# The attention's 1 / rms on GpSimd: one power operation in place of eleven Newton-step operations

## Chip, core and metric

The kernel runs on one core of a Trainium2 chip. The metric is the device time of the whole program in microseconds. A core has five engines with queues of their own: TensorE (PE in the profile, its weight loads PEld), VectorE (DVE), ScalarE (ACT), GpSimd (POOL) and SyncE (SP, which here issues every DMA). Each engine works through its queue in order and waits on semaphores where it needs another's result.

## What is computed

A linear attention, whose normalised output goes through a gated MLP that mixes tokens. Eight batches of 576 tokens; 8 heads of 64 channels, so 512 channels; the MLP is 512 to 1024 to 512.

```
kv   = einsum('bhsd,bhse->bhde', k, v)
out  = einsum('bhsd,bhde->bhse', q, kv)
rms  = sqrt(mean(out * out, axis=-1) + 1e-06)
x    = out / rms * g_norm                     # heads joined to 512 channels
h    = gelu(x @ w_in);  u, v = halves of h
v_n  = layer_norm(v) * g_ln
v_s  = einsum('ts,bsd->btd', w_sg, v_n) + b_sg[None, :, None]
y    = x + (u * v_s) @ w_out
```

## The kernel before

Matrices are multiplied in float32 quality from two parts: a rounded high part (names ending in h) and a rest (ending in o). `split` makes them: ScalarE casts the high part, VectorE or GpSimd subtracts to get the rest. A product is then three matmuls, high by high, high by rest and rest by high.

Each batch b has an attention object `Att` and an MLP object `Moe`. Attention: `kv` sums key by value over five chunks of tokens in the PSUM tile pkv; `o` makes po for each pair of heads, squares it (sq, ScalarE) and scales it by g into x; `sums` adds the squares per head with a matmul by a matrix of ones into pss; `rstd` turns pss into ry, the 1 / rms, 128 partitions by 144. Batch 0 spreads ry over the channels on TensorE: `scale_pe` makes yh and y_parts and then eight matmuls pb, whose results multiply x. The other batches write ry to DRAM (rd) and read it back broadcast (bc for 512 tokens, bl for the last 64), and `scale` and `xleft` multiply x with them. `xsplit` makes xh and xo.

MLP: `v` makes pv, gelu (hv), layer norm and its parts vh and vo; its 1 / sigma, rs, is an addition and a power on GpSimd, on 128x1, with the exponent tile mhalf (-0.5). `uu` makes pu and u. `s_main` and `s_left` make pg, the token mix; VectorE scales it into gt, GpSimd multiplies it with u, and it is split into gh and go. `out` makes py and adds it to x. Weights w_in and w_out are 64-bit words that are converted on chip (`w64`, tiles "words" and w64: ScalarE L164, VectorE L166 to L168, GpSimd's addition L169, and a split); w_u, w_v, w_out give wuh/wuo, wvh/wvo, woh/woo, and ws the token-mixing weights wsh/wso.

The work is written down step by step in the lists FIRST (batch 0 with all weight work and batch 1's attention), ODD, EVEN, LAST_EVEN and LAST; in each, step r (or F, or T for later batches) is `rstd` of this or the next batch. The list is not the queues' order: the framework's scheduler lays the instructions of all engines out by its own simulated clock, and the queues follow that. The tiles rm, ry and ra have one buffer each, shared by all batches.

Of the kernel before, what the change touches and what calls it, by code (L numbers as in the profile page):

```python
# [9 lines left out]
I32 = mybir.dt.int32  # L10
U32 = mybir.dt.uint32
AF = mybir.ActivationFunctionType
ALU = mybir.AluOpType

P = 128
B, H, S, D = 8, 8, 576, 64
# [7 lines left out]
QS = S // NQ  # L24
ZO = H - 2
RMS_EPS = 1e-6
LN_EPS = 1e-6
MAGIC = 0x5F3759DF
# [43 lines left out]
def tile_linear_attn_gmlp(  # L72
# [18 lines left out]
    nc = tc.nc  # L91
# [4 lines left out]
    def T(shape, dtype, tag, bufs=1, nm=None):  # L96
        return sb.tile(shape, dtype, tag=tag, bufs=bufs, name=nm or tag)
# [21 lines left out]
    mhalf = T([P, 1], F32, "mhalf")  # L119
# [65 lines left out]
    class Att:  # L185
# [106 lines left out]
        def rstd(self):  # L292
            m = T([P, QS], F32, "rm")
            y = T([P, QS], F32, "ry")
            a = T([P, QS], F32, "ra")
            v = nc.vector
            v.tensor_scalar(m, self.pss[:, :QS], D * RMS_EPS, None, op0=ALU.add)
            v.tensor_scalar(a.bitcast(I32), m.bitcast(I32), 1, None, op0=ALU.logical_shift_right)
            v.tensor_scalar(y.bitcast(I32), a.bitcast(I32), -1.0, float(MAGIC), op0=ALU.mult, op1=ALU.add)
            for _ in range(3):  # L300
                v.tensor_tensor(a, y, y, op=ALU.mult)
                v.scalar_tensor_tensor(a, a, -0.5, m, op0=ALU.mult, op1=ALU.mult)
                v.scalar_tensor_tensor(y, a, 1.5, y, op0=ALU.add, op1=ALU.mult)
            if self.b == 0:
                self.y = y
            else:
                self.rd = dr.tile([32, S], F32, tag="rd", name="rd")
                nc.sync.dma_start(self.rd.rearrange("h (j t) -> j h t", j=NQ), y)
# [342 lines left out]
```

## Time and profile before

| | |
|---|---|
| median of 2 runs | 562.2 us (561.58 to 562.82) |
| profiled execution | 561.72 us |
| its span | 559.9 us, 9943 instructions |
| mean granted TensorE clock | 0.982 |
| DMA traffic | 55.50 MB |

Engine rows of the profile give busy us, share of the span and instructions. Group rows give line, engine, operation, tiles out<-in with shapes and count, then busy us and mean ns of one, then the engine's idle time before them. Timeline rows give start us, duration us, engine, line, operation. Rows of a line or tile give least/median/greatest ns of one operation. Rows of a stretch give from:to, its length, the busy us (and count) of PE, PEld, DVE, ACT and POOL, the granted clock, the DMA engines' share and GB/s. Rows of the chain that ended last give start us, duration us, engine, tile, line and count.

### The profile page before, as it was taken

The page shows a single profiled execution, that of the slowest core. Times are in us where ns is not written, and L with a number is a line of the kernel's source. Part 1 is how long each engine was busy: PE and PEld are TensorE (multiplying, and loading weights), DVE is VectorE, ACT ScalarE, POOL GpSimd, SP SyncE. Part 2 cuts the span into 40 slices and gives each one's busy share as a digit, 9 for nine tenths or more (in the row PEclk, how much of TensorE's full clock was granted, in tenths as well). Part 3 has the DMA queues.
Part 4 walks back from the last instruction along what each step waited for, and adds up shares of the span by engine and source line. Part 5 has one row for each costly group of instructions (what it writes and reads, how often), then busy time and mean ns, then how long its engine had stood idle before and what let it go on. Part 6 is the DMA issues. An engine that isn't in the chain of part 4 may idle for free.

```text
span 559.9 us, 9943 instructions
## 1 busy us (share of the span) xinstructions
PE 523.3 (93%) x3944; PEld 469.3 (84%) x3944; DVE 305.6 (55%) x644; ACT 200.5 (36%) x457; POOL 196.3 (35%) x221
## 2 busy tenths in 40 slices
PE   2878957999999999899999999999999999999997
PEld 2556756888998988898998989988898979989997
DVE  0689989834645263844634353663652444762443
ACT  1446636432434332342414352332513342421210
POOL 1217667341249022422248131331328312430221
PEclk9979979999999999999999999989999999999999
DMA  8996556332023302513044312613242202102002
GB/s 221 293 332 189 164 160 165 116 100 86 22 70 85 123 28 64 162 32 128 22 134 110 127 43 53 188 39 108 60 115 73 85 1 53 37 2 85 1 1 86
DMA packets 33723, 55.50 MB, mean 99 GB/s; under 512 B 7308, under 2 KB 9228, under 8 KB 33676
## 3 DMA queue, kind: packets, MB, share of 16 engines
q1 hardware_dynamic: 33676, 54.86, 32.6%
q8 instruction: 31, 0.51, 0.4%
q14 instruction: 16, 0.13, 0.1%
HBM read 44.90 MB, written 9.95 MB: 98 GB/s over the span
## 4 chain that ended last, share of the span: by engine, by line
PE 61%; DVE 15%; DMA 13%; POOL 4%; ACT 2%; issue 2%; SPq 2%; POOLq 0%; DVEq 0%
PE py L454 18%; PE pv L386 13%; PE pu L413 12%; PE pg L427 10%; DMA bc<-rd 5%; PE po L266 4%; DMA kv_first<-in_kx 3%; PE pss L281 2%; DVE xo L111 2%; DVE go L111 2%; SPq L314 2%; DMA rd<-ry 1%; POOL x L321 1%; PE pkv L220 1%; DVE words L166 1%
## 5 line engine op out<-in xcount | busy, mean ns | idle before, releaser
L440 POOL TENSOR_TENSOR gt<-gt,u 128x288 f32<-128x288 f32 x64 | 55.6, 884 | 93.8 <-DVE gt L439 85.3
L427 PE MATMUL pg<-wsh,vh 128*128 128x288 f32 x256 | 77.5, 305 | 1.8 <-ACT vh L110 1.8
L454 PE MATMUL py<-go,woh 128*128 128x288 f32 x256 | 75.5, 299 | 2.2 <-DVE go L111 2.1
L454 PE MATMUL py<-gh,woh 128*128 128x288 f32 x256 | 73.0, 304 | 4.1 <-ACT gh L110 3.8
L427 PE MATMUL pg<-wso,vh 128*128 128x288 f32 x256 | 75.9, 299 | 0.0
L427 PE MATMUL pg<-wsh,vo 128*128 128x288 f32 x256 | 74.0, 299 | 1.6 <-DVE vo L111 1.6
L454 PE MATMUL py<-gh,woo 128*128 128x288 f32 x256 | 74.8, 296 | 0.0
L376 POOL TENSOR_SCALAR rs<-mv 128x1 f32<-128x1 f32 x32 | 9.8, 307 | 144.3 <-DVE mv L375 144.1
L111 DVE TENSOR_TENSOR go<-gt,gh 128x288 fp32r<-128x288 f32 x64 | 40.0, 638 | 28.2 <-ACT gh L110 28.2
L457 DVE SCALAR_TENSOR_TENSOR x<-py,x 128x288 f32<-128x288 f32 x64 | 28.2, 454 | 45.2 <-PE py L454 45.0
L427 PEld LDWEIGHTS pg<-wsh,vh 128*128 128x128 f32 x256 | 49.0, 192 | 4.3 <-ACT vh L110 2.4
L454 PEld LDWEIGHTS py<-gh,woh 128*128 128x128 f32 x256 | 46.6, 189 | 7.2 <-ACT gh L110 5.0
L413 PE MATMUL pu<-xh,wuh 128*128 128x288 f32 x256 | 48.0, 305 | 4.2 <-ACT hv L370 3.7
L454 PEld LDWEIGHTS py<-go,woh 128*128 128x128 f32 x256 | 48.5, 189 | 3.4 <-DVE go L111 3.3
L427 PEld LDWEIGHTS pg<-wsh,vo 128*128 128x128 f32 x256 | 48.1, 192 | 2.7 <-DVE vo L111 2.3
L439 DVE SCALAR_TENSOR_TENSOR gt<-pg,glt,b_bc 128x288 f32<-128x288 f32 x64 | 30.8, 511 | 34.6 <-PE pg L437 34.1
L427 PEld LDWEIGHTS pg<-wso,vh 128*128 128x128 f32 x256 | 49.3, 193 | 0.3
L454 PEld LDWEIGHTS py<-gh,woo 128*128 128x128 f32 x256 | 48.6, 190 | 0.0
L413 PE MATMUL pu<-xh,wuo 128*128 128x288 f32 x256 | 46.1, 298 | 2.3 <-POOL wuo L111 2.3
L413 PE MATMUL pu<-xo,wuh 128*128 128x288 f32 x256 | 46.3, 299 | 1.6 <-DVE xo L111 1.6
L416 ACT ACTIVATE u<-pu 128x288 f32<-128x288 f32 x64 | 26.2, 411 | 60.0 <-PE pu L413 59.9
L110 ACT CAST gh<-gt 128x288 fp32r<-128x288 f32 x64 | 26.9, 434 | 57.1 <-POOL gt L440 42.6
(117 smaller groups left out, 1076.8 us busy)
## 6 DMA issues: line engine op xcount, KB each, us to landing
q<-in_qT SPq DMA_DIRECT2D x32, 288.0 KB, 3.5
out_y<-x SPq DMA_DIRECT2D x28, 288.0 KB, 2.1
bc<-rd SPq DMA_DIRECT2D x28, 256.0 KB, 4.3
k<-in_kx SPq DMA_DIRECT2D x24, 256.0 KB, 4.1
v<-in_vx SPq DMA_DIRECT2D x24, 256.0 KB, 4.3
kv_first<-in_kx SPq DMA_DIRECT2D x8, 256.0 KB, 7.2
kv_first<-in_vx SPq DMA_DIRECT2D x8, 256.0 KB, 8.4
words<-in_wu SPq DMA_DIRECT2D x4, 512.0 KB
```

What stands on the lines that cost most here:

```text
L110: nc.scalar.copy(hi, src)
L111: return (lo_engine or nc.vector).tensor_tensor(lo, src, f32(hi), op=ALU.subtract)
L266: nc.tensor.matmul(po[:, :HS], a, m[:, t], start=(i == 0), stop=(i == len(terms) - 1))
L281: nc.tensor.matmul(self.pss[32 * j : 32 * j + m, :QS], ones[:, ZO - 2 * p : ZO - 2 * p + m], self.sq[p, j // 2][:, j % 2 * QS : (j % 2 + 1 ...
L386: nc.tensor.matmul(pv, a(cc), w[:, cc, :], start=(n == 0), stop=(n == 11))
L413: nc.tensor.matmul(pu[:, :HS], w[:, cc, f], a[cc][:, t], start=(n == 0), stop=(n == 11))
L416: nc.scalar.activation(u, pu[:, :HS], AF.Gelu_apprx_tanh, scale=W_UP)
L427: nc.tensor.matmul(ps[:, :HS], a[:, d], w[:, c, t], start=(n == 0), stop=False)
L439: nc.vector.scalar_tensor_tensor(gt, ps[:, :HS], glt[:, dc : dc + 1], b_bc[:, t], op0=ALU.mult, op1=ALU.add)
L440: nc.gpsimd.tensor_tensor(gt, gt, self.u.pop((j, dc)), op=ALU.mult)
L454: nc.tensor.matmul(po[:, :HS], w[:, dc, f], a, start=(i == 0), stop=(i == 11))
L457: nc.vector.scalar_tensor_tensor(x[:, t], po[:, :HS], W_UP, x[:, t], op0=ALU.mult, op1=ALU.add)
```

## The change

`rstd` keeps its first operation (VectorE adds the epsilon to pss, giving rm). The other eleven go: two that make a first guess from the bits, and three Newton steps of three operations each. One GpSimd operation raises rm to the power -0.5, with the one-column tile mhalf broadcast along 144.

```
             v = nc.vector
-            v.tensor_scalar(m, self.pss[:, :QS], D * RMS_EPS, None, op0=ALU.add)
-            v.tensor_scalar(a.bitcast(I32), m.bitcast(I32), 1, None, op0=ALU.logical_shift_right)
-            v.tensor_scalar(y.bitcast(I32), a.bitcast(I32), -1.0, float(MAGIC), op0=ALU.mult, op1=ALU.add)
-            for _ in range(3):
-                v.tensor_tensor(a, y, y, op=ALU.mult)
-                v.scalar_tensor_tensor(a, a, -0.5, m, op0=ALU.mult, op1=ALU.mult)
-                v.scalar_tensor_tensor(y, a, 1.5, y, op0=ALU.add, op1=ALU.mult)
+            nc.vector.tensor_scalar(m, self.pss[:, :QS], D * RMS_EPS, None, op0=ALU.add)
+            nc.gpsimd.tensor_tensor(y, m, mhalf.to_broadcast([P, QS]), op=ALU.pow)
             if self.b == 0:
                 self.y = y
```

The scheduler lays out the whole program anew with this. Lines behind the edit have numbers lower by five. On VectorE, at the start of the program, behind batch 0's rm there stood the Newton steps, then yh and y_parts:

```order
L302 SCALAR_TENSOR_TENSOR ra<-ra,rm 128x144
L237 COPY kvf<-pkv 64x4x64
L303 SCALAR_TENSOR_TENSOR ry<-ra,ry 128x144
L328 CAST yh<-ry 128x144
L331 SCALAR_TENSOR_TENSOR y_parts<-yh,ext,ry 32x144 x4
```

Now, from batch 1's kvf on:

```order
L166 TENSOR_SCALAR words<-words 128x256
L168 SCALAR_TENSOR_TENSOR w_522<-words,w_522 128x256
L167 TENSOR_SCALAR w_542<-w_542 128x256
L168 SCALAR_TENSOR_TENSOR w_542<-words,w_542 128x256
L242 TENSOR_TENSOR kvo<-pkv,kvh 64x4x64
L323 CAST yh<-ry 128x144
L297 TENSOR_SCALAR rm<-pss 128x144
L242 TENSOR_TENSOR kvo<-pkv,kvh 64x4x64
L326 SCALAR_TENSOR_TENSOR y_parts<-yh,ext,ry 32x144 x4
L167 TENSOR_SCALAR w_460<-w_460 128x512
L335 TENSOR_TENSOR x<-x,pb 128x288
```

Twelve weight conversions (the last four of them shown; w_522 and w_542 are of w_out, w_460 of w_v) and the first half of batch 2's kvo now stand ahead of yh, and batch 1's rm right behind it.

On GpSimd, at the start, the weight additions and x splits were:

```order
L111 TENSOR_TENSOR wuo<-w_382,wuh 128x2x256
L169 TENSOR_TENSOR w_428<-w_428,words 128x512
L169 TENSOR_TENSOR w_470<-w_470,words 128x512
L111 TENSOR_TENSOR xo<-x,xh 128x576 x2
L169 TENSOR_TENSOR w_495<-w_495,words 128x512
```

and are now (ry is the power, of batch 0 and of batch 1):

```order
L298 TENSOR_TENSOR ry<-rm,mhalf 128x144
L111 TENSOR_TENSOR wuo<-w_372,wuh 128x2x256
L169 TENSOR_TENSOR w_418<-w_418,words 128x512
L169 TENSOR_TENSOR w_522<-w_522,words 128x256
L169 TENSOR_TENSOR w_542<-w_542,words 128x256
L298 TENSOR_TENSOR ry<-rm,mhalf 128x144
L169 TENSOR_TENSOR w_460<-w_460,words 128x512
L111 TENSOR_TENSOR xo<-x,xh 128x576
L111 TENSOR_TENSOR wso<-stage,wsh 128x576 x2
L111 TENSOR_TENSOR xo<-x,xh 128x576
```

Both powers stand ahead of the second w_v addition and of batch 0's x splits. In a later odd batch (3) VectorE's order around rm is, with buffer numbers, now:

```order
L373 TENSOR_SCALAR hv_2135<-hv_2135,mv_2138,rs_2139 128x512
L297 TENSOR_SCALAR rm_2186<-pss_2117 128x144
L369 BN_STATS st_2162<-hv_2160 128x6
L111 TENSOR_TENSOR vo_2051<-hv_2135,vh_2050 128x512
L370 BN_AGGR mv_2163<-st_2162 128x2
L369 BN_STATS st_2337<-hv_2335 128x6
L370 BN_AGGR mv_2338<-st_2337 128x2
L373 TENSOR_SCALAR hv_2160<-hv_2160,mv_2163,rs_2164 128x512
```

and on GpSimd rs_2164, for which the last row waits, stands behind the power (before, no GpSimd operation belonged to `rstd`, and the Newton steps stood between these rows on VectorE).

## Prediction

> **What bounds the kernel now.** I read the page's busy shares first, then the slices, then a table of stretches.
>
> ```profile
> PE 523.3 (93%) x3944; PEld 469.3 (84%) x3944; DVE 305.6 (55%) x644; ACT 200.5 (36%) x457; POOL 196.3 (35%) x221
> PE   2878957999999999899999999999999999999997
> 25.00:57.00 32.00, 26.83 (x248) 18.68 (x249) 29.93 (x56) 18.40 (x45) 15.46 (x11) 0.89 0.81 258
> 57.00:105.00 48.00, 38.35 (x249) 31.78 (x249) 44.02 (x85) 25.42 (x55) 29.36 (x29) 0.93 0.53 150
> 130.00:560.00 430.00, 419.78 (x3122) 387.38 (x3120) 212.21 (x459) 142.08 (x328) 137.96 (x163) 0.99 0.24 71
> ```
>
> There are two regimes. From 130 us on TensorE (PE) is busy 419.78 of 430 us: it sets the time, and VectorE (DVE, the third pair) is half idle. From 25 to 105 us DVE is the full engine (29.93 of 32, 44.02 of 48 us) and PE idles 5.2 + 9.7 us. So a relief of DVE is worth something before 105 us only; after that the change matters by whether it makes PE wait.
>
> **What goes.** Of twelve DVE operations per batch on 128x144 one stays.
>
> ```profile
> L302 DVE SCALAR_TENSOR_TENSOR ra<-ra,rm 128x144 f32<-128x144 f32 x24 | 9.5, 398 | 0.7
> L301 DVE TENSOR_TENSOR ra<-ry 128x144 f32<-128x144 f32 x24 | 7.8, 324 | 0.7
> L303 DVE SCALAR_TENSOR_TENSOR ry<-ra,ry 128x144 f32<-128x144 f32 x24 | 7.8, 324 | 0.7
> L298 DVE TENSOR_SCALAR ra<-rm 128x144 int32<-128x144 int32 x8 | 3.6, 447 | 0.1
> L299 DVE TENSOR_SCALAR ry<-ra 128x144 int32<-128x144 int32 x8 | 1.8, 229 | 0.2
> ```
>
> That is 9.5 + 7.8 + 7.8 + 3.6 + 1.8 = 30.5 us of DVE, 3.8 us a batch. In six of eight batches PE's own work covers it: worth nothing.
>
> **What comes: the duration P of one power operation.** No row shows it at 128x144. The layer norm has one on 128x1.
>
> ```profile
> L376 POOL TENSOR_SCALAR rs<-mv x32: 214/223/1445, 77.3 to 523.3; 128x1 f32<-128x1 f32 x32
> L377 POOL TENSOR_TENSOR rs<-rs,mhalf x32: 557/568/1007, 77.7 to 523.6; 128x1 f32<-128x1 f32 x32
> L440 POOL TENSOR_TENSOR gt<-gt,u x64: 793/812/1327, 105.0 to 549.4; 128x288 f32<-128x288 f32 x64
> L321 POOL TENSOR_TENSOR x<-x,bc x22: 1277/1297/1815, 81.8 to 486.1; 128x512 f32<-128x512 f32 x22
> ```
>
> The columns are least, median and greatest ns. Two multiplications give (1297 - 812)/224 = 2.17 ns an element a partition, and 812 - 288 x 2.17 = 0.19 us of fixed cost; an addition on one element takes 0.22. So one power on one element costs 0.57 - 0.22 = 0.35 us more than an addition. Lower end: all of that is paid once, P = 0.57 + 143 x 0.00217 = 0.9 us. Upper end: all of it is paid for each element, P = 0.22 + 144 x 0.35 = 50 us. The nearest row is the power itself, whose 0.35 us holds both a first-time part and the element's latency, which a loop over 144 can partly overlap. I choose a third of it an element, 0.12 us: **P = 0.22 + 144 x 0.12 = 17.5 us**. This is a choice inside a wide bracket, and nearly all the width below comes from it.
>
> **The power also shuts out DVE.** DVE operations that read PSUM never stretch; those with only SBUF operands do, beside a POOL operation.
>
> ```profile
> L272 DVE TENSOR_SCALAR x<-po,g x20: 501/516/518, 19.4 to 455.4; 128x288 f32<-128x288 f32 x20
> L378 DVE TENSOR_SCALAR hv<-hv,mv,rs x32: 533/546/1792, 79.2 to 524.2; 128x512 f32<-128x512 f32 x32
> 27.41 1.27 POOL L111 TENSOR_TENSOR wuo<-w,wuh 128x512 fp32r<-128x512 f32 x1 [0.73 <-ACT wuh L110]
> 27.91 0.86 DVE L298 TENSOR_SCALAR ra<-rm 128x144 int32<-128x144 int32 x1
> ```
>
> The shift at 27.91 us, 0.23 us where nothing is beside it, ended at 28.77, just after POOL's operation (28.68): it waited for the whole of it. The Trainium skill, SBUF — State Buffer, "SBUF: two separate sides", states it: the port pair shared by GpSimd and VectorE is locked for a full instruction and the loser waits. The trace agrees (0.86 against 0.23 us), and by it a power of 17.5 us holds such DVE operations for up to 17.5 us; were the port shared evenly, the even batches' term below would shrink by some 3 us each.
>
> **Start of the program (batches 0 and 1).** Batch 0's result feeds the first useful PE work through y_parts and the eight pb matmuls.
>
> ```profile
> 27.59 0.29 DVE L297 TENSOR_SCALAR rm<-pss 128x144 f32<-128x144 f32 x1
> 34.97 0.85 PE L338 MATMUL pb<-y_parts,heads 128*128 128x288 f32 x1
> 35.87 0.45 DVE L340 TENSOR_TENSOR x<-x,pb 128x288 f32<-128x288 f32 x1
> 45.75 0.91 SPq L148 DMA_DIRECT2D words<-in_wo  x2
> 54.47 0.42 SPq L206 DMA_DIRECT2D k<-in_kx  x1
> 45.21 1.64 DVE L166 TENSOR_SCALAR words<-words 128x512 int32<-128x512 uint32 x1
> 54.85 1.76 DVE L111 TENSOR_TENSOR wvo<-w,wvh 128x512 fp32r<-128x512 f32 x1
> 41.17 0.33 SPq L206 DMA_DIRECT2D k<-in_kx  x1
> L331 DVE SCALAR_TENSOR_TENSOR y_parts<-yh,ext,ry 32x144 fp32r<-32x144 f32 x4 | 1.4, 360 | 0.1
> k<-in_kx SPq DMA_DIRECT2D x24, 256.0 KB, 4.1
> ```
>
> In the changed order yh stands on DVE behind twelve weight conversions, two of them of the first w_out words, and behind the first kvo, which needs all of batch 2's keys. Those arrive by DMA whatever P is. The w_out words were issued at 45.75 us; the last k chunk at 54.47, queued behind w_in words and a stage load, most of which now come later. I put its issue at 46 us (an estimate: it needs the buffer of the chunk that was issued at 41.17, a little earlier now, once PE has summed it) and its landing 4.1 us later, at 50. With PE's sums, ACT's cast, kvo, yh, rm and four y_parts (0.36 us each) pb then starts at about 54.5 us instead of 34.97. This hides the first power, which starts at 27.9, while P stays under about 15 us; beyond that the SBUF-only conversions in front wait for it, and they take about 9.5 us with POOL's additions between them (from 45.21 to 54.85 us DVE did as many such operations): at P = 17.5 pb comes at 45.4 + 9.5 + 2, some 2.5 us later still.
>
> The second power follows as soon as y_parts has been read, since both batches use one buffer each for rm and ry. Behind it on POOL stand the addition for w_v, the x splits xo (two), four ws splits and the other w_v additions; on DVE the next SBUF-only conversion is locked out and the pb products stand behind that. Before, this stretch took 20.7 us from 35.87 to the end of the last wvo at 56.61; now it takes P plus about 22 from 54.5. Its end moves by 54.5 + P + 22 - 56.6 = 20 + P. Two credits: PE has done all of batch 1's attention and batch 2's kv sums by then (some 5 us of matmuls), and of the 9.7 us that PE idled between 57 and 105 I count 8 as no longer idle, because weight work was pulled ahead and batch 1's Newton steps are gone. **Start: 20 + 17.5 + 2.5 - 13 = +27 us.**
>
> **Batches 2 to 7.** Here the question is how much PE work, independent of POOL, follows the last pss. The rates, and the first links behind pss:
>
> ```profile
> 132.56 2.74 PE pv L386 x12
> 142.36 1.60 PE pu L413 x12
> 159.87 1.57 PE pg L427 x12
> 113.53 1.22 PE pkv L220 x30
> 149.13 0.36 PE pss L281 x8
> 149.55 0.31 DVE L297 TENSOR_SCALAR rm<-pss 128x144 f32<-128x144 f32 x1 [0.34 <-PE pss L281]
> L111 DVE TENSOR_TENSOR vo<-hv,vh x32: 653/692/1507, 84.7 to 525.4; 128x512 fp32r<-128x512 f32 x32
> ```
>
> Even-numbered batches (2, 4, 6): the changed order has 61 pg, 48 pu, 48 pkv, 14 po and 8 pss matmuls before the first py that needs a product made behind the power: 8.0 + 6.4 + 2.0 + 1.8 + 0.4 = 18.6 us (po at pu's rate). The chain is rm (0.34 + 0.31 us), P, two gt products (0.8 each), ACT's cast and the hand-overs (1.1 as an estimate): P + 3.4. PE waits P - 15.2 = 2.3 us.
>
> Odd-numbered batches (3, 5, 7): the second vo split of SBUF operands stands on DVE right behind rm, so it is locked out until the power ends, and PE needs it after 60 pu, 12 pv and 5 pg: 8.0 + 2.7 + 0.7 = 11.4 us. It comes after rm (0.65), P, itself (0.69) and a hand-over: P + 1.5. PE waits P - 9.9 = 7.6 us. The two rs chains behind the power on POOL end soon after and stay covered.
>
> A long wait costs again in clock:
>
> ```profile
> 75.30:78.95 3.65, 0.00 (x0) 0.00 (x0) 3.50 (x10) 2.70 (x7) 1.05 (x2) 0.56 0.80 223
> 78.95:82.00 3.05, 3.05 (x13) 3.05 (x13) 1.44 (x3) 1.25 (x3) 1.19 (x2) 0.50 1.07 220
> ```
>
> After 3.65 us without matmuls the granted clock was 0.50 for about 3 us: some 1.7 us lost. I count it for the three long waits and once at the start: 6 us. **Batches 2 to 7: 3 x 2.3 + 3 x 7.6 = 30, and 6 for the clock.** Nothing in them is late for the DMAs of rd and bc, whose readers lie over 35 us of PE work behind pss.
>
> **Sum.** The profiled execution took 561.72 us (span 559.9 plus 1.8), 0.5 below the median of the two runs. 561.7 + 27 + 30 + 6 = 625; I give **625 us**.
>
> **Rivals.**
>
> 1. *The power streams.* P about 0.9 us. Then no wait in batches 2 to 7, and at the start 20 + 0.9 - 13 = +8: 570 us, within 2%. For it: POOL's multiplications do stream at 2.17 ns an element. Against: 0.57 against 0.22 us on a single element. The Trainium skill, GPSIMD Engine Reference, "Elementwise — side-by-side cycle accounting", has two-input elementwise work at about 2.6 cycles an element; if that held for the power too, this rival would be the result. The multiplications agree with it (2.17 ns), the power on one element tells nothing of its slope. The 2% line (573) is crossed at P of about 4 us.
>
> 2. *The power is nearly serial,* P = 30 us. The first power then ends at 58 and delays pb to 69 (+15); start 20 + 30 + 15 - 13 = +52; even batches 14.8 and odd 20.1 us each, 105; clock 12: 731 us. The full upper end, P = 50, would give near 890.
>
> 3. *The relief of DVE wins,* not slower: if the rows ahead of yh are ready early (k and w_out words landed by about 40 us) and P is below 4 us, pb moves hardly, and DVE, full from 25 to 105 us, gives up the Newton steps of two batches there, 2 x 3.8 us, which PE's 14.9 idle us can return: 554 us, and less where a step had stretched beside POOL. For it: DVE's 44.02 of 48 us. Against: the k chunk's issue at 54.47 us is far from 40, and yh stands behind its sums in any case. It decides at a landing before about 42 us together with a small P.
>
> 4. *The order doesn't bite.* The same split is fed but PE's order absorbs even a 17.5 us power, so that only the start counts: 561.7 + 27 + 2 = 591 us. It lies inside my forecast's own range.
>
> **How the numbers follow.** My forecast, P between 4 and 28 us: 0.58, times from 574 to about 715. Power streams: 0.15. Nearly serial: 0.20. Relief wins: 0.07, of it 0.04 beyond 2%. That the change doesn't do what it says has no room: the order shows one power for eleven steps. 2% is about what a measurement of this kernel can tell from no change. Faster 0.04, same 0.18, slower 0.78. The range reaches from the streaming power's low side, 567, to a P of 31 us, 740; beyond lie the relief below and the dearest powers above, some 0.2 together.
>
> **What would show it.** The mean of the power's own group gives P at once. Right: DVE's SBUF-only operations that start beside a power last nearly as long as it; pb starts at 50 to 60 us; PE's waits in the odd batches end on vo, in the even ones on gh or go; granted clock below 1 after them. Wrong: a P under 4 us with pb still at 54 us (then only the order costs), pb near 35 us (then my reading of the order failed), or waits that end on bc.

## Result: 691 us, 23% slower

The changed kernel takes 691.35 us (median of two runs, 688.76 and 693.93) against 562.2: 1.230 times, with a 95% interval of 1.209 to 1.250. I had predicted 625 us, in a range of 567 to 740. The direction held; the increase is 129 us where I had 63. The profiled execution is the one of 693.93 us (span 692.2).

The page of the changed kernel, busy shares and two rows of slices:

```profile
PE 560.4 (81%) x3944; PEld 498.0 (72%) x3944; DVE 283.0 (41%) x556; ACT 203.5 (29%) x457; POOL 382.6 (55%) x229
PE   3875167999977797689996689489995989489998
PEclk9965569999997899799998879799998889799999
```

TensorE (PE) does the same 3944 matmuls but is busy 37 us longer, nearly all of it at the lower clock (worked out below under the clock), and it idles 95 us more (692.2 - 560.4 = 131.8 against 559.9 - 523.3 = 36.6). 37 + 95 is the whole difference. The holes in its row of slices come at regular distances over all eight batches. The stretches:

```profile
25.00:57.00 32.00, 22.37 (x224) 12.70 (x221) 11.16 (x27) 11.83 (x29) 28.63 (x7) 0.71 0.87 280
57.00:112.00 55.00, 26.14 (x93) 20.54 (x93) 35.36 (x58) 18.98 (x43) 49.78 (x22) 0.61 0.32 94
130.00:690.00 560.00, 482.01 (x3421) 440.59 (x3419) 216.78 (x428) 157.40 (x357) 291.68 (x181) 0.92 0.21 61
```

At the start GpSimd (POOL, the fifth pair) is now the full engine, 49.78 of 55 us, and VectorE is relieved as the change wanted (35.36). Behind 130 us PE works 482 of 560 us at a clock of 0.92; before it was 420 of 430 at 0.99.

**The power itself,** its group, and the two at the start with what stands behind the second (timeline of POOL, then PE):

```profile
L298 POOL TENSOR_TENSOR ry<-rm,mhalf 128x144 f32<-128x144 f32 x8 | 187.1, 23388 | 12.3 <-DVE rm L297 10.6 <-DVE y_parts L326 1.7
27.95 23.33 POOL L298 TENSOR_TENSOR ry<-rm,mhalf 128x144 f32<-128x144 f32 x1 [1.27 <-DVE rm L297]
56.85 23.48 POOL L298 TENSOR_TENSOR ry<-rm,mhalf 128x144 f32<-128x144 f32 x1 [1.71 <-DVE y_parts L326]
81.53 1.40 POOL L111 TENSOR_TENSOR xo<-x,xh 128x576 fp32r<-128x576 f32 x1
55.98 0.61 PE L333 MATMUL pb<-y_parts,heads 128*128 128x288 f32 x1 [3.00 <-DVE y_parts L326]
82.99 1.81 PE L408 MATMUL pu<-xo,wuh 128*128 128x288 f32 x6 [16.81 <-POOL xo L111]
```

P is 23.3 us, eight times: 187 us of GpSimd for 30 us of VectorE. As foreseen, pb starts late, at 56.0 us, and hides the first power, and the second holds up xo behind it: the longest single wait of the program, 16.81 us.

**An odd batch (3),** POOL and PE:

```profile
256.90 23.32 POOL L298 TENSOR_TENSOR ry<-rm,mhalf 128x144 f32<-128x144 f32 x1 [1.00 <-DVE rm L297]
280.30 0.51 POOL L371 TENSOR_SCALAR rs<-mv 128x1 f32<-128x1 f32 x2
280.89 1.18 POOL L372 TENSOR_TENSOR rs<-rs,mhalf 128x1 f32<-128x1 f32 x2
282.74 0.61 PE L422 MATMUL pg<-wsh,vh 128*128 128x288 f32 x1 [9.74 <-ACT vh L110]
282.70:286.00 3.30, 3.26 (x13) 3.26 (x14) 1.31 (x2) 0.61 (x1) 0.00 (x0) 0.50 0.24 56
```

The two layer-norm chains (rs) stand behind the power; hv, vh and then pg wait for them. PE waits 9.74 us and then starts at half clock (last row, a stretch).

**An even batch (2)** waits by another way. The chain that ended last, from 204 to 240 us:

```profile
204.58 4.69 DMA v<-in_vx
209.41 1.14 PE pkv L220 x16
210.56 0.33 SPq L206
210.94 0.42 SPq L207
211.42 5.14 DMA rd<-ry
218.57 4.12 DMA bc<-rd
226.04 4.06 DMA bc<-rd
230.23 2.52 POOL x L316 x2
237.78 7.06 PE py L449 x32
```

One chunk of v lands, PE sums it, that frees a buffer, SyncE's queue (SPq) issues the next k and v loads and only then rd, which had been behind them; then bc, the x products on POOL, and py. The power does not stand in this piece. That was the first hint that the order, not the power alone, costs time. The list of PE's waits says it too; the list of before has no wait for this v (the tile of batches 2 to 7) at all:

```profile
PE pkv L220 <- DMA v<-in_vx: 20.0, 13, 3.6
```

### The profile page after: what moved, and what is told of

It is laid out like the page before. It is cut to its first block, busy times and chain, and to the rows that moved or that the text cites. A ratio compares the mean times of both kernels' runs of the same rounds, so it can differ in the third digit from the quotient of the medians.

```text
span 692.2 us, 9860 instructions
## 1 busy us (share of the span) xinstructions
PE 560.4 (81%) x3944; PEld 498.0 (72%) x3944; DVE 283.0 (41%) x556; ACT 203.5 (29%) x457; POOL 382.6 (55%) x229
## 4 chain that ended last, share of the span: by engine, by line
PE 50%; DMA 16%; issue 12%; POOL 10%; DVE 7%; ACT 3%; SPq 2%; POOLq 0%; DVEq 0%; ACTq 0%
PE py L449 13%; PE pv L381 10%; PE pg L422 10%; PE pu L408 9%; POOL ry L298 7%; DMA bc<-rd 4%; DMA v<-in_vx 4%; DMA kv_first<-in_vx 3%; PE po L266 3%; PE pkv L220 2%; DMA rd<-ry 2%; POOL x L316 2%; PE pss L281 1%; DVE go L111 1%; DMA q<-in_qT 1%
## 5 line engine op out<-in xcount | busy, mean ns | idle before, releaser
L298 POOL TENSOR_TENSOR ry<-rm,mhalf 128x144 f32<-128x144 f32 x8 | 187.1, 23388 | 12.3 <-DVE rm L297 10.6
L422 PE MATMUL pg<-wsh,vh 128*128 128x288 f32 x256 | 82.0, 322 | 30.3 <-ACT vh L110 27.5
L449 PE MATMUL py<-gh,woh 128*128 128x288 f32 x256 | 77.9, 324 | 22.9 <-ACT gh L110 18.0
L449 PE MATMUL py<-go,woh 128*128 128x288 f32 x256 | 80.2, 317 | 1.6 <-DVE go L111 1.6
L422 PE MATMUL pg<-wso,vh 128*128 128x288 f32 x256 | 80.0, 314 | 0.0
L422 PEld LDWEIGHTS pg<-wsh,vh 128*128 128x128 f32 x256 | 53.0, 207 | 33.2 <-ACT vh L110 28.2
L449 PEld LDWEIGHTS py<-gh,woh 128*128 128x128 f32 x256 | 50.7, 206 | 27.1 <-ACT gh L110 19.2
L111 DVE TENSOR_TENSOR go<-gt,gh 128x288 fp32r<-128x288 f32 x64 | 47.4, 759 | 51.3 <-ACT gh L110 51.3
L316 POOL TENSOR_TENSOR x<-x,bc 128x512 f32<-128x512 f32 x22 | 30.1, 1382 | 50.4 <-DMA bc<-rd 48.0
L408 PEld LDWEIGHTS pu<-xo,wuh 128*128 128x128 f32 x256 | 40.2, 199 | 21.1 <-POOL xo L111 20.9
```

The costliest lines, as they stand in the source:

```text
L111: return (lo_engine or nc.vector).tensor_tensor(lo, src, f32(hi), op=ALU.subtract)
L298: nc.gpsimd.tensor_tensor(y, m, mhalf.to_broadcast([P, QS]), op=ALU.pow)
L316: engine.tensor_tensor(xs, xs, self.pair[p // 2][:, p % 2, :], op=ALU.mult)
L408: nc.tensor.matmul(pu[:, :HS], w[:, cc, f], a[cc][:, t], start=(n == 0), stop=(n == 11))
L422: nc.tensor.matmul(ps[:, :HS], a[:, d], w[:, c, t], start=(n == 0), stop=False)
L449: nc.tensor.matmul(po[:, :HS], w[:, dc, f], a, start=(i == 0), stop=(i == 11))
```

## The experiments

To tell order from power, several kernels keep one and change the other. The scheduler lays out the queues by a table of operation times; in these kernels a copy stands in the power's place (ry is then rm, so the root is left out), and its entry in that table is set to the power's:

```
-            nc.gpsimd.tensor_tensor(y, m, mhalf.to_broadcast([P, QS]), op=ALU.pow)
+            nc.gpsimd.tensor_copy(y, m)
...
+    setattr(_spec, table, {**prices, "TensorCopy": prices["Pow"]})
```

So the program is ordered as for a power, but waits for none. On TensorE and SyncE this order is the changed kernel's, row for row; on the three other engines the traces differ by the eight copies for the eight powers, and by three operations that stand in another place (two casts on ScalarE, one addition on VectorE). Times of before were 558.2 to 561.1 us beside these runs; ratios go to that.

### The power, the port and the clock by themselves

> A kernel of its own that leaves the attention and the MLP out: powers of several sizes on GpSimd, a chain of VectorE operations with SBUF operands beside one power, beside fourteen multiplications and by itself, and bursts of matmuls after waits of about 2 to 15 us. Theory: the power is a loop, 0.16 us an element of a partition: 3.1 us at 18 columns, 5.9 at 36, 11.8 at 72, 23.3 at 144, 46 at 288, and the same on 32 partitions; VectorE keeps its own pace beside a power (within 5% of the chain by itself), is stretched beside the multiplications, and after waits of 8 us and more the granted clock is 0.50 for some 10 us. Rival 1: the 23.3 us hold a fixed part or come from the other engines' traffic, so that 72 columns take well over 12 us or a power alone is much shorter than 23. Rival 2 (my prediction's): GpSimd locks VectorE out for the whole instruction, so that one operation of the chain lasts some 20 us.

Groups of this kernel: the power by size, then the VectorE chain's products beside a power (powtt) and alone; the last two rows are of the timeline, the first multiplication and a product that starts beside it (multt):

```profile
L41 POOL TENSOR_TENSOR y<-rm,mhalf 128x1 f32<-128x1 f32 x1 | 0.6, 555 | 0.0
L41 POOL TENSOR_TENSOR y<-rm,mhalf 128x72 f32<-128x72 f32 x1 | 11.8, 11839 | 0.0
L41 POOL TENSOR_TENSOR y<-rm,mhalf 128x144 f32<-128x144 f32 x1 | 23.3, 23290 | 0.0
L41 POOL TENSOR_TENSOR y<-rm,mhalf 128x288 f32<-128x288 f32 x1 | 46.2, 46208 | 0.0
L43 POOL TENSOR_TENSOR yrows<-rm,mhalf 32x144 f32<-32x144 f32 x1 | 23.3, 23285 | 0.0
L58 DVE TENSOR_TENSOR powtt<-powtt,rs 128x512 f32<-128x512 f32 x9 | 6.3, 703 | 0.3
L58 DVE TENSOR_TENSOR alonett<-alonett,rs 128x512 f32<-128x512 f32 x4 | 2.8, 692 | 0.1
188.28 1.77 POOL L72 TENSOR_TENSOR mula<-gateb,rs 128x512 f32<-128x512 f32 x1 [0.81 <-DVE gateb L69]
188.96 1.63 DVE L58 TENSOR_TENSOR multt<-multt,rs 128x512 f32<-128x512 f32 x1
```

The power behaves as a plain loop: (46.21 - 23.29)/144 = 0.159 us an element and some 0.4 us besides, the same on 32 partitions and with the other compute engines idle beside it. Rival 1 falls. Rival 2, mine, falls as well: beside a power VectorE's two-operand products keep 703 ns against 692 alone, while each of the five that start beside a multiplication takes 1630 ns. (The other four of that chain come when the multiplications are over, and take 690 again.) The clock part of the expectation was misread. PE's six waits were 2.2 to 18.2 us; the records have one stretch at 0.50 for each, 3.4 to 17.1 us long, but most of a long one lies in the wait itself. PE was busy 3.2 to 6.1 us in each, and about as long behind 18.2 us (3.5) as behind 2.2 (3.4). Two stretches behind the last wait, which ended at 423.1 us:

```profile
424.00:426.50 2.50, 2.50 (x4) 1.01 (x3) 0.00 (x0) 0.00 (x0) 0.50 0.00 0
426.50:430.00 3.50, 3.50 (x9) 1.52 (x8) 0.00 (x0) 0.00 (x0) 0.98 0.00 0
```

So each of these six waits cost 1.6 to 3 us of clock, whatever its length. The Trainium skill, TensorE: Matmul & The Clock Gate, "Part 1: The HAM clock gate (the "warmup" mystery)", says that the first 3.4 us or so of work run at half rate; the runs agree behind four of the waits (3.2 to 3.9 us) and have more behind the other two (4.5 and 6.1).

### The order alone, and half a power in it

> The changed kernel's order, with a plain copy of rm in the power's place (the root is left out). Theory (P, the duration of the power, is the cost): the order by itself costs only the later start, 20 + 0.5 - 13 = +8 us, so 565 to 580 us. Rival (the new order is the cost, with twelve conversions and the first kvo ahead of yh and other products behind pss): 600 us or more.

> The changed kernel's order, with the power on 72 of the 144 columns and a copy on the others. Theory: P is 11.8 us, below what the order covers in the batches 2 to 7 (17 us behind pss in odd ones, 15 in even ones), so only the start pays, 20 + 12 - 13 = +19 us: 575 to 595 us. Rival (cost in proportion to the power, since every power is waited for in full): half of 129 us, near 626.

The second kernel raises 72 columns and copies the others, with the same planned total:

```
+ nc.gpsimd.tensor_copy(y[:, QS // 2 :], m[:, QS // 2 :])
+ nc.gpsimd.tensor_tensor(y[:, : QS // 2], m[:, : QS // 2], ..., op=ALU.pow)
```

Measured: 628.18 us with the copy (1.121, interval 1.117 to 1.126) and 631.35 with half a power (1.129, 1.124 to 1.134). The theory fell in the first and the rival was right: **the order alone costs 68 us, more than half of the 129**, with no power anywhere. The second lies outside the theory's 575 to 595 too, and near the rival's 626, but that is a coincidence: the rival had every power waited for, and half a power costs only 3 us more here than none. So 11.8 us of power are hidden nearly everywhere, and what lies above, from 11.8 to 23.3, costs the other 60 (691 less 631). The copy kernel has the even batches' chain of above with no power in it:

```profile
187.10 4.78 DMA v<-in_vx
194.03 4.48 DMA rd<-ry
200.52 4.92 DMA bc<-rd
213.00 2.53 POOL x L316 x2
```

### What VectorE's relief is worth

> A plain copy in the power's place (the root is left out), and the order planned for the copy: what the relief of VectorE alone is worth. Theory: 3.8 us of VectorE a batch are beside TensorE's work in the batches 2 to 7 and worth nothing; at the start at most the two batches' 7.6 us come back: 554 to 564 us. Rival (VectorE is worth more than that): below 552 us.

The copy, planned as a copy: 570.19 us, 1.018 (1.014 to 1.022) of before, above the theory's range. Eleven VectorE operations a batch fewer, no power, and it is not faster but 10 us slower. Its layout is new as well: PE waits 8.4 us for v and 4.6 us for u in it, two waits that before doesn't have. The run doesn't separate the relief from the layout; together they bring nothing, and the 554 us of my third rival did not come.

### Planned for a power in some batches, or for half of one

The first two set the copy, planned as a power, under a condition on the batch, with a multiplication planned as such elsewhere; the third halves the planned time.

> Cheap operations in the power's place everywhere (root left out), but the order is planned for a power in batches 0 and 1 only. Theory (the order's 68 us split as the trace of the cheap run has them, 16 by the end of batch 0's MLP and some 45 behind it, each made by the batches that are planned so): 570 + 16 = 586 us (578 to 594). Rival (the weights moved at the start upset the later stages too): 605 us or more.

> Cheap operations everywhere (root left out), the order planned for a power in batches 2 to 7 only. Theory: 570 + 45 = 615 us (606 to 622), with K steps in a row that wait for their k and v loads. Rival: 590 us or less.

> A copy in the power's place (root left out), planned as if it took half the power's time, 11.8 us. Theory (the planner fills the time for which it holds GpSimd with work that then runs out or waits for its loads, in proportion to it): half of the 58 us between the copy planned as a copy (570) and as a power (628), near 599 us (588 to 610). Rival (11.8 us are covered, by the slacks of 9.9 and 15.2 us that I counted, so that the plan for them differs little): 565 to 580 us.

587.92 (1.054), 607.81 (1.090) and 599.20 us (1.075). All three lie in the theory's ranges. The parts add up: 1.054 + 1.090 - 1.018 = 1.126 against 1.121 measured for both. So planning for the power costs 20 us at the start and 40 us in batches 2 to 7 (ratios less that of the copy planned as a copy, by 560), and half the planned time costs half.

### How the plan's lateness costs: five runs

> As the run with a copy in the power's place (root left out), planned as if the copy took the power's time, but with three buffers for k and v instead of two (the unused ra makes the room). In that run batch 2's rd was issued 28 us behind ry (194.0 against 166), behind k and v loads that waited for their buffers on the same queue, and POOL's x products and the gt products behind them waited for bc. Theory S (this queue is what the order costs in the batches 2 to 7, 42 of its 68 us in the two stages of batches 1 and 3): rd is issued within 10 us of ry, most of the 42 comes back, 585 to 600 us. Rival (the loads only fill a wait that another part of the order makes): 618 to 632 us.

620.32 us (1.108): the rival's number. The third buffer moved rd hardly, since the loads ahead of it on SyncE wait for PE's sums and for a q split; but the waits for v fell by 12 us, here against the copy kernel with two buffers (first row), and the time by 8:

```profile
PE pkv L220 <- DMA v<-in_vx: 21.7, 11, 3.9
PE pkv L220 <- DMA v<-in_vx: 9.5, 8, 2.2
```

> The root is left out: VectorE writes ry itself, and a copy that nobody reads stands on GpSimd, planned as if it took the power's time. So the plan still holds GpSimd for a power, but ry is early in it. Theory S2 (the order costs 68 us because all that reads ry is planned late: yh and pb at the start, rd and bc with what stands behind them later): with ry early nearly all of it goes, 565 to 585 us. Rival (the planned hold of GpSimd, by which rs chains and gt products are put elsewhere, is the cost): 615 to 632 us, as with the late ry (628).

> As the run with ry early in the plan, but only in batches 2 to 7; batches 0 and 1 keep the late ry (root left out everywhere). Theory S2: the start keeps its 15 us and the later stages lose their some 50: 575 to 592 us. Rival (planned hold): 615 to 632 us; and if the start alone were the cause, 628.

624.21 (1.112) and 627.38 us (1.118). Theory S2 fell by a test that did what it was to do: with ry early in the plan, batch 2's rd goes out right behind ry instead of 28 us later, and pb starts at 29.4 us instead of 53.4,

```profile
170.36 0.59 SPq L303 DMA_DIRECT2D rd<-ry  x1
29.39 0.37 PE L333 MATMUL pb<-y_parts,heads 128*128 128x288 f32 x1 [0.40 <-DVE y_parts L326]
PE pkv L220 <- DMA v<-in_vx: 22.5, 10, 3.5
PE pv L381 <- ACT wvh L110: 17.6, 1, 17.6
```

and the program is hardly faster (4 us, then 1, against the copy kernel's 628). The waits have only moved: at the start to w_v's conversion, whose VectorE steps now stand behind batch 1's products with bl, and in the later batches PE still waits 22.5 us for v. So the cost comes with a plan that takes GpSimd as held for 23 us, whether ry is late in it or early.

> A copy in the power's place, planned with the power's time (root left out), and rd, bl and bc issued by GpSimd's own queue, so that rd stands right behind ry and not behind the k and v loads of SyncE's queue. Theory S (that queue is where the late ry costs in batches 2 to 7): rd within 1 us of ry, 628 goes to 585 to 605 us. Rival (the products that read bc are late in the order whatever the queue): 618 to 632 us.

> The changed kernel in full, with rd, bl and bc issued by GpSimd's queue. Theory S: in even batches rd goes 5 us earlier (ry ends at 206.5, rd was issued at 211.4 us in batch 2) and k and v no longer stand behind a rd that waits; GpSimd in turn waits 4 to 5 us for rd's landing before bc: some 10 us less than 691, 670 to 690. Rival (the power on GpSimd is all that counts): 691 or more, since GpSimd is given yet more to do.

608.51 (1.084, interval 1.076 to 1.091) and 685.23 us (1.221, 1.214 to 1.228). The first is between theory and rival and says little of its own question: the plan put other work between ry and rd on GpSimd too (ry at 170.3, rd at 188.9 us), so that rd was not close behind. The 20 us came with a different layout. With the real power, the 685 us lie in the theory's range, but also within the interval of the unchanged 691, so they decide nothing.

### The real power, part by part, in the fixed order

> The changed kernel's order, the real power in batches 3, 5 and 7 only, a copy in the others (their root is left out). Theory: in odd batches the rs chain stands behind the power, a wait of 9.7 us and about 2.5 us of clock for each, so 628 + 3 x 12 = 664 us (658 to 670), and the even batches and the start are worth the rest of 691. Rival (all eight powers cost alike, 63/8 = 7.9 each): 652 us.

> The changed kernel's order, the real power in batches 0 and 1 only, a copy in the others (their root is left out). Theory: the second power holds up the x splits on GpSimd for 17 us at the start and costs nothing later: 628 + 17 = 645 us (640 to 652). Rival (a later start shifts everything and later waits absorb it): 628 to 635 us.

661.29 us (1.182) and 642.86 us (1.149). Both as the theory said: 34 us for the three odd batches, 11.3 each, and 16 us for the start. In the odd run the wait is that of the changed kernel:

```profile
266.62 0.61 PE L422 MATMUL pg<-wsh,vh 128*128 128x288 f32 x1 [9.76 <-ACT vh L110]
```

What is left to the even batches is 1.230 - 1.121 - 0.061 - 0.028 = 0.020, some 11 us, uncertain by as much, since the changed kernel's own interval is 2% to either side, and only if the parts add up.

### The power without its plan

> The changed kernel's computation in full, but planned as if the power took a multiplication's time, so that the order is close to that of the copy planned as a copy (570 us). Theory (the planned lateness costs 68 us but saves more, since without it each power is waited for nearly in full): the first power is no longer hidden, some 38 us at the start; 15 to 20 us in each of six batches and 30 us of clock: 735 us (700 to 770). Rival (the order made for the power costs as much as it saves): 690 us or less.

750.51 us (1.342, interval 1.335 to 1.349), above the 735 that I gave and inside its bounds. PE's three largest sums of waits:

```profile
PE pg L422 <- DVE gt L434: 63.2, 3, 21.5
PE pv L381 <- ACT xlh L110: 28.0, 3, 21.9
PE pb L333 <- DVE y_parts L326: 23.8, 1, 23.8
```

Each power is waited for nearly whole: PE's timeline has eight waits of 18.6 to 23.8 us, one for each. So the order that costs 58 us over one planned for a copy saves some 60 over an unprepared one: it is a price paid for the power, not a fault of its own.

## Why the prediction was wrong, step by step

All in us; the last column from the ratios above by 560.

| step | predicted | measured |
|---|---|---|
| P, one power | 17.5 | 23.3 |
| pb's start (behind weights and kvo) | 54.5, 57 with the hold of VectorE | 56.0 |
| start: order and power together | 27 | 20 + 16 |
| odd batches, with their clock | 23 + 5 | 34 |
| even batches | 7 | 11, uncertain |
| order of batches 2 to 7, without any power | 0 | 40 |
| a new layout as such (with VectorE's relief in it) | 0 | 10 |

- **P was mis-sized.** I took a third of the power's extra time on one element for each further element, 0.12 us; it is 0.159. The bracket (0.9 to 50) held it. With 23.3 us my own sum would have been 561.7 + 39 + 24 + 40 + 6 = 671: two thirds of the miss. That it comes so near is partly luck. At 23.3 us its terms for the odd batches with their clock and for the even ones are 45 and 24, where 34 and some 11 were measured, and this excess stands in for part of the 50 us (the last two rows) that I had at nothing.
- **The step that failed is the order of batches 2 to 7.** I counted, for each parity, the PE work between pss and the first product made behind the power, and took the rest of the new order as free ("Nothing in them is late for the DMAs of rd and bc"). The cover is there: half a power costs 3 us more than none. But the same order costs 40 us in these batches with no power in it. Against the copy planned as a copy, the plan for a power in batches 2 to 7 alone lengthens the profiled execution by 37 us: PE idles 26.5 us more, and is busy 10.5 us longer at a lower clock. Its waits for v, gh and gt (first three rows) are the largest that grew; the copy planned as a copy has the last two, and no wait of pg for gt:

```profile
PE pkv L220 <- DMA v<-in_vx: 16.8, 11, 3.5
PE py L449 <- ACT gh L110: 8.8, 5, 3.8
PE pg L422 <- DVE gt L434: 6.1, 2, 3.3
PE pkv L220 <- DMA v<-in_vx: 8.4, 3, 3.7
PE py L449 <- ACT gh L110: 2.0, 3, 1.1
```

The runs show that the 40 us come from planning GpSimd as held, and that the order's whole cost grows with the planned time (29 us for half of it, 58 for all); which moved rows make up the 40 beyond these waits stays open, since the five runs aimed at it changed more than one thing or left the time as it was. My fourth rival, that the order absorbs the power, had the same blind spot.
- **The lock of VectorE was wrong for a power.** I had it hold VectorE's SBUF operations for the whole instruction, as they are beside its other operations. In the changed kernel they keep their quiet times beside a power: first the very vo split that I had locked out in batch 3, which starts 0.4 us into the power of 256.90 us (0.69 us by itself), then a split beside the second power:

```profile
257.34 0.67 DVE L111 TENSOR_TENSOR vo<-hv,vh 128x512 fp32r<-128x512 f32 x1
59.26 0.68 DVE L111 TENSOR_TENSOR wvo<-w,wvh 128x512 fp32r<-128x512 f32 x1
```

The Trainium skill, SBUF — State Buffer, "SBUF: two separate sides", says that the pair is locked for the whole instruction; beside multiplications the runs agree (1630 against 692 ns), beside a power they do not (703 against 692), and the measurement decides. (My own row for the lock shows a little less than a full hold: the shift ended 0.09 us behind GpSimd's operation, and takes 0.23 by itself.) My odd batches came out near the right size by luck: the way was not vo but the rs chains, which I had called covered. Their sum is P + 3.7 against 17.0 us of PE work, 10.0 at P = 23.3, where 9.74 was measured.

- **The clock.** I took 1.7 us for a wait; behind the 9.74 us wait PE was busy 5.1 us at 0.50, a loss of 2.5. The count was further off: I had four waits, the trace has fourteen stretches at 0.50, one of them of 54.6 us at the start, where waits of 1.8 to 16.8 us follow one another. Short waits count too: in the kernel with the six waits the half clock took 3.4 us of work behind 2.2 us, and 3.5 behind 18.2. Half of PE's busy time inside the fourteen stretches is 44 us, against 8 before: 36 where I had 6. The measured rows of the table contain it.
- **Right were** the place of pb, the second power ahead of xo, the sign of every term that I had, and that VectorE's relief would not win.

The Trainium skill, GPSIMD Engine Reference, "Elementwise — side-by-side cycle accounting", with about 2.6 cycles an element, does not speak for a power: 0.159 us an element is some 70 times the 2.17 ns of the multiplications.

## What to carry to other kernels

Before an operation moves to an engine on which it has run at one size only, its slope is what must be known: a single row at 128x1 left a factor of fifty open. A saving on an engine that is half idle brought nothing here, and a long operation on a queue that others share was paid twice, since a scheduler planned for it: once for what it still delays, and once for the order that makes room for it; a cheap stand-in, planned at the dear one's time, told the two apart.

## What the hardware showed beside that

A GpSimd power takes 0.159 us for each element of a partition, on 32 partitions as on 128 (23.285 against 23.290 us at 144 columns), and leaves VectorE undisturbed (703 against 692 ns) although a GpSimd multiplication more than doubles the same VectorE operation (1630 ns). The granted clock fell to 0.50 for each of six waits from 2.2 to 18.2 us, and the half clock behind them lasted 3 to 6 us of work, 3.4 us behind 2.2 us and 3.5 behind 18.2; so in this range the number of the waits sets what they cost in clock, not their length.
